# Hedgehog linear attention on one core: K and Q weights folded together, and another order of the first loads

## The chip, the cores and the metric

The kernel runs on one core of one Trainium2 chip, in one launch. The metric is the device time of the core in microseconds (us). Its engines are TensorE (PE, with its weight loads shown as PEld), VectorE (DVE), ScalarE (ACT), GpSimd (POOL) and SyncE (SP). SP only issues transfers in this kernel; POOL issues four more (the head weights). The transfers of a core share 16 DMA engines.

## The reference

Two branches, A and B, run over the same input x (2048 tokens, 448 channels, 16 heads of 28) and are mixed by a gate. For each branch:

```python
q, k, v = split((x @ wqkv), 3)                     # 16 heads of 28
pq, pk = q @ w_phi[h], k @ w_phi[h]                # 28x28 for each head
phi_q = concat(softmax(pq), softmax(-pq))          # 56 features
phi_k = concat(softmax(pk), softmax(-pk))
kv, z = phi_k.T @ v, phi_k.sum(tokens)
o = (phi_q @ kv) / (phi_q @ z + 1e-6)
branch = o @ wo
out = g * branch_A + (1 - g) * branch_B            # g = sigmoid(x . gate_w)
```

All is float32. x and the weights reach TensorE as a high part and a low part (the value rounded, and what the rounding left), and three of the four products are summed.

## The kernel before, in words

The 2048 tokens are 16 tiles of 128; two tiles make a pair of x. A projection half (one tile, one of the two branches b) is 11 matmuls: 448 channels are three chunks of 128 and one of 64, and the last chunk carries the low part of x in its upper half. So V of a tile is 22 matmuls, K 22, Q 22.

K and Q are never projected with the raw weights. The head matrices `w_phi` are first multiplied into the raw K and Q weights ("fold"), so that x times the folded weights gives pk and pq at once. `load_wt` loads the transposed raw weights of K or Q of a branch in four transfers, one for each partition quarter (28 partitions each, four runs of 2 KB per partition). `fold` multiplies four groups of heads in 32x32 tiles of the array into the four PSUM banks F, DVE transposes F (L338) to `ft`, ACT casts four column blocks to the high part (`rk` for K, `rq` for Q), and DVE or POOL subtracts the low part.

`steps()` writes the order of the work out by hand. It sets the order of TensorE strictly; for all other engines a planner (class `Plan`) takes each step with its cost, latency and `ahead` and lets every engine take the most urgent step that is ready. The planner counts no more than eight transfers in flight. What it emits is then fixed: every engine runs its instructions in order. At the start the steps are

- `V01`: V of tiles 0 and 1, the terms taken as weights arrive (`v_first`, L413; tile 1 uses the bank of K),
- `FK` 0, x of pair 1 (`x1`), V of tile 2, `FK` 1, loads of the raw Q weights (`wq`), V of tile 3, x of pair 2,
- `FQ` 0 and 1 with V of tile 4, K of tiles 0 and 1, then a loop over pairs: K, Q, `S` (softmax of Q in another layout, by a round trip through DRAM), `kv` (L467, sums K features times V), V of the pair after.

After the loop come the products with `kv` and the output projection (L597). The loads before all this, in SP's queue: x of pair 0 (512 KB), eight V weight chunks (225 KB each, `load_wv`), four raw K loads, x of pair 1, four raw K loads, x of pair 2, eight raw Q loads. Ten warm-up matmuls and thirty small ones (L606 and L609) run ahead of everything. `split_x` and `split_wv` make the high part on ACT (L269) or DVE and the low part on DVE or POOL (L266). `load_wp` brings the head weights `wp` by POOL. `k_soft` makes the K features: ACT copies K from PSUM to `pk`, DVE takes maxima and sums, POOL subtracts and scales. `hand_over` makes one buffer's users wait for another's.

Memory is shared in time: the raw V weights, x of pair 1 and the raw Q weights lie in `re`, which later holds the K features; the raw K weights lie in `rt`, later the Q features.

## Time and profile before

| what | value |
|---|---|
| median of 3 runs | 344.81 us |
| lowest and highest run | 343.89, 345.26 us |
| span of the profiled execution, first to last instruction | 343.6 us |
| TensorE busy | 333.2 us (97%) |
| DVE, POOL, ACT busy | 283.8, 241.0, 145.3 us |
| granted clock of TensorE | 0.999 |
| moved by DMA | 55.21 MB, mean 161 GB/s |

The profiled execution's own device time is not listed beside its span; the times of the runs lie 0.3 to 1.7 us above that span.

In the profile a line such as `L380 PE MATMUL K<-rk,rx 128*128 128x432 f32 x22` names the kernel's line, the engine, the operation, the output and inputs, the shapes and the count; in the timeline it has start and length in us ahead of it, and in brackets the idle time before it with what ended that. In a table by stretch, each engine's busy time stands with its count of instructions, then the granted clock, the share of the 16 DMA engines that was busy, and GB/s. In the chain of waits each row has start, length and who held the chain.

### The profile page before, as it was taken

To read this page: it belongs to the slowest core of one execution; us is meant where nothing else is said; L and a number is where in the kernel's file an instruction comes from. 1 tells how busy PE (TensorE), PEld (TensorE's weight loads), DVE (VectorE), ACT (ScalarE), POOL (GpSimd) and SP (SyncE) were. 2 spreads that over 40 slices of the span, in tenths; PEclk is the share of its full clock that TensorE was granted. 3 is DMA by queue.
4 is the path that set the end of the run, shared out by engine and by line. 5 is a ranking of instruction groups with operands and counts; after the bars stand their busy time and mean duration, and the time that the engine had idled before them with its cause. 6 is when DMAs were issued, how large, how long until landed. Compare 5 with 4: busy or idle time off the path is not lost.

```text
span 343.6 us, 9382 instructions
## 1 busy us (share of the span) xinstructions
PE 333.2 (97%) x4032; PEld 298.5 (87%) x4032; DVE 283.8 (83%) x342; ACT 145.3 (42%) x219; POOL 241.0 (70%) x195
## 2 busy tenths in 40 slices
PE   7979999999999999999999999999899999999995
PEld 6857799899999999999999999999688888888895
DVE  3548788897987979879899799986699999999870
ACT  4527665444444526446236344242043343433231
POOL 3003287999999969997987986895088678788400
PEclk9999999999999999999999999999999999999999
DMA  7998720650477486386446332377955644241011
GB/s 243 223 193 184 208 74 27 189 170 1 110 280 211 136 306 213 113 259 245 129 117 246 97 80 86 94 265 246 317 191 192 202 156 164 93 175 56 30 53 53
DMA packets 29488, 55.21 MB, mean 161 GB/s; under 512 B 4304, under 2 KB 23248, under 8 KB 27144
## 3 DMA queue, kind: packets, MB, share of 16 engines
q1 hardware_dynamic: 29320, 54.52, 51.0%
q8 instruction: 31, 0.51, 0.6%
q0 software_dynamic: 128, 0.12, 0.1%
q14 instruction: 9, 0.07, 0.1%
HBM read 32.00 MB, written 24.22 MB: 164 GB/s over the span
## 4 chain that ended last, share of the span: by engine, by line
PE 91%; DMA 5%; issue 1%; ACT 1%; SPq 1%; POOL 0%; POOLq 0%; ACTq 0%
PE K L380 20%; PE O L597 20%; PE Q L380 20%; PE VA L380 10%; PE VB L380 9%; PE N L549 6%; PE T L467 4%; DMA re<-in_xt 4%; PE F L334 2%; DMA re<-in_wv 2%; SPq L272 1%; ACT rx L269 0%; POOL re L266 0%; ACT re L269 0%; POOLq L266 0%
## 5 line engine op out<-in xcount | busy, mean ns | idle before, releaser
L380 PE MATMUL Q<-rq,rx 128*128 128x432 f32 x352 | 72.2, 359 | 1.1 <-issue 1.1
L380 PE MATMUL K<-rk,rx 128*128 128x432 f32 x352 | 72.2, 360 | 0.0
L597 PE MATMUL O<-rk,rx 128*128 128x448 f32 x336 | 70.4, 368 | 0.0
L380 PEld LDWEIGHTS Q<-rq,rx 128*128 128x128 f32 x352 | 66.0, 188 | 4.7 <-issue 1.2
L597 PEld LDWEIGHTS O<-rk,rx 128*128 128x128 f32 x336 | 62.6, 188 | 8.1 <-issue 1.6
L380 PEld LDWEIGHTS K<-rk,rx 128*128 128x128 f32 x352 | 65.9, 188 | 3.4 <-issue 0.2
L266 POOL TENSOR_TENSOR re<-re,sm 128x896 f32<-128x896 f32 x32 | 53.9, 1707 | 7.6 <-DVE sm L456 7.4
L269 ACT ACTIVATE re<-re 128x896 f32<-128x896 f32 x32 | 30.5, 953 | 31.9 <-POOL re L266 31.7
L455 DVE TENSOR_REDUCE sm<-re 128x32 f32<-128x896 f32 x32 | 33.8, 1071 | 4.4 <-ACT re L269 4.4
L266 POOL TENSOR_TENSOR rt<-qmn,ru 128x896 f32<-128x896 f32 x16 | 28.2, 1764 | 11.7 <-DMA ed<-rt 7.3
L380 PE MATMUL VA<-rv,rx 128*128 128x450 f32 x154 | 34.5, 372 | 1.4 <-ACT rx L269 1.4
L507 DVE TENSOR_REDUCE qsm<-rt 128x32 f32<-128x896 f32 x32 | 33.5, 1056 | 0.6 <-ACT rt L269 0.4
L380 PE MATMUL VB<-rv,rx 128*128 128x448 f32 x154 | 33.5, 365 | 0.0
L269 ACT ACTIVATE rt<-ru 128x896 f32<-128x896 f32 x16 | 15.3, 953 | 40.7 <-issue 17.3
L380 PEld LDWEIGHTS VA<-rv,rx 128*128 128x128 f32 x154 | 28.5, 189 | 4.5 <-ACT rx L269 1.7
L380 PEld LDWEIGHTS VB<-rv,rx 128*128 128x128 f32 x154 | 29.0, 188 | 2.3
L512 DVE STREAM_TRANSPOSE rt<-rt 128x2048 f32<-128x2048 f32 x13 | 29.6, 2278 | 1.6 <-POOL rt L266 1.5
L266 POOL TENSOR_TENSOR re<-pk,mx 128x896 f32<-128x896 f32 x16 | 27.9, 1746 | 2.7 <-DVE mx L448 2.7
L266 POOL TENSOR_TENSOR rt<-rt,qsm 128x896 f32<-128x896 f32 x16 | 27.3, 1705 | 0.9
L266 POOL TENSOR_TENSOR re<-mx,pk 128x896 f32<-128x896 f32 x16 | 27.3, 1704 | 0.0
L269 ACT ACTIVATE pk<-K 128x896 f32<-128x896 f32 x16 | 14.8, 922 | 29.3 <-PE K L380 29.3
L569 POOL TENSOR_TENSOR rv<-rv,rd 128x896 f32<-128x896 f32 x14 | 23.9, 1704 | 1.1
(96 smaller groups left out, 462.9 us busy)
## 6 DMA issues: line engine op xcount, KB each, us to landing
ed<-rt SPq DMA_DIRECT2D x8, 1024.0 KB
qd<-ru SPq DMA_DIRECT2D x64, 112.0 KB
ru<-qd SPq DMA_DIRECT2D x16, 448.0 KB
re<-ed SPq DMA_DIRECT2D x5, 1024.0 KB
xraw<-in_xt SPq DMA_DIRECT2D x7, 512.0 KB
out<-re SPq DMA_DIRECT2D x16, 224.0 KB
wod<-wst SPq DMA_DIRECT2D x14, 224.0 KB
rk<-wod SPq DMA_DIRECT2D x2, 1568.0 KB
```

The source lines that it names most:

```text
L266: return lambda: ENG[eng].tensor_tensor(val(o), val(a), val(b), op)
L269: return lambda: A.activation(val(o), val(i), f, **k)
L272: return lambda: nc.sync.dma_start(o, i)
L334: nc.tensor.matmul(bank["F"][32 * o:32 * o + 32, q, g * P:(g + 1) * P], wpd[32 * q:32 * q + DH, b, g], wts[k][b][32 * q:32 * q + DH, g].re ...
L380: nc.tensor.matmul(bank[name][:, k, lo:hi], x[:, xc, o:o + P], w[l][:, c], start=i == 0, stop=i == len(XT) - 1)
L455: put("DVE", 2 * D, lambda s=s, e3=e3: V.tensor_reduce(sm[:, s], e3, AX.X, OP.add), [ke[s]], [("sm", t % 2, s)])
L467: nc.tensor.matmul(kvp()[32 * r:32 * r + DH + 1, b, g], vs[t % NV][:, b, h // 2, h % 2], es[t % NE][:, :, hs:hs + DH], start=(t == 0 and b ...
L507: put("DVE", 2 * D, lambda s=s, e3=e3: V.tensor_reduce(qsm[:, s], e3, AX.X, OP.add), [ke[s]], [("qsm", i, s)])
L512: add("DVE", 2.25, lambda: V.transpose(eTf[slot], eq.rearrange("p s a c f -> p (s a c f)")), ke, turned(slot))
L549: nc.tensor.matmul(bank["N"][32 * g:32 * g + 32, r, 2 * b * P:2 * b * P + 2 * P], kvt[32 * r:32 * r + 32, b, s, g], eTp[slots[0] // 2][32 ...
L569: put(eng, 2 * D, lambda: ENG[eng].tensor_tensor(mid["o", n % 3].rearrange("p (c a f) -> p a c f", c=4, a=8), ctv()[:, :, i, :, :DH], rd[: ...
L597: nc.tensor.matmul(bank[pb][:, 0, :D], a, w, start=i == 0, stop=i == len(terms) - 1)
```

## The change

- Raw K and Q weights are folded together. A fold now takes one branch b and every second head group (gh): its matmuls have 256 moving columns, 128 of K and 128 of Q. There are still four folds, of half as many matmuls. Each fold makes K's and Q's high and low parts; K's are given priority on ACT, and low parts alternate between DVE and POOL.
- The transfers of the raw weights of partition quarters 0 and 1 stay on SP's queue, those of quarters 2 and 3 go on ACT's queue and start after the last V chunk is cast. K and Q weights of branch 0 are loaded first, then those of branch 1. `rt` and `re` become one tile `ret`, so that the raw weights of both lie in one range.
- x of pair 0 is loaded as chunk 0, then (after the first V chunk) chunks 1 to 3, and split by chunks on ACT, DVE and POOL. `v_first` takes its 11 terms in another order.
- x of pair 1 is split on ACT with one low half on DVE and one on POOL; its load comes ahead of the raw weights. x of pair 2 is split by POOL alone.
- The head weights come in eight transfers instead of four.
- The bank of K is tracked by halves; tile 0's K output is copied in two halves. K of tile 3 runs ahead of kv(0,1). The second half of V of tile 4 runs ahead of K of tile 0.

The diff, cut to its core:

```diff
-    yield from (("V01", 0, 0, 1), ("V01", 1, 0), ("V01", 1, 1), ("FK", 0), ("x1",), ("V", 2), ("FK", 1), ("wq", 0), ("wq", 1), ("V", 3), ("x", 2))
-    yield from (("FQ", 0), ("V", 4, 0), ("FQ", 1), ("later",), ("K", 0), ("V", 4, 1), ("K", 1), ("wo_rows",))
-    yield from (("Q", 0), ("S", 0, JIT % 3 - 1), ("K", 2), ("Q", 1), ("S", 1, (JIT - 1) % 3 - 1), ("kv", 0, 1), ("K", 3), ("V", 5))
+    yield from (("V01", 0, 0, 1), ("x1",), ("V01", 1, 0), ("V01", 1, 1), ("wq", 0), ("x", 2), ("wq", 1), ("V", 2, 0), ("F", 0, 0), ("V", 2, 1), ("F", 0, 1))
+    yield from (("V", 3, 0), ("F", 1, 0), ("V", 3, 1), ("V", 4, 0), ("F", 1, 1), ("later",), ("V", 4, 1), ("K", 0), ("K", 1), ("wo_rows",))
+    yield from (("Q", 0), ("S", 0, JIT % 3 - 1), ("K", 2), ("Q", 1), ("S", 1, (JIT - 1) % 3 - 1), ("K", 3, 0), ("kv", 0, 1), ("K", 3, 1), ("V", 5))
...
+    def load_x0():
+        for i, (lo, hi) in enumerate(((0, 1), (1, 4))):
+            if i:
+                load_wv(0, 0)
+            add("SP", 0.4, dma(xraw[:, lo:hi], xd[lo * P:hi * P, :2 * P].rearrange("(c p) t -> p c t", p=P)), [], [("x0raw", i)], lat=3, kb=184 * (hi - lo), ahead=60.0 - 20 * i)
+
+    def split_x0():
+        n, t, f = 0, xs[0], xs[0].bitcast(F32)
+        h, l = [[(k, n, i) for i in range(2)] for k in ("x", "xl")]
+        put("ACT", 2 * P, act(t[:, 0], xraw[:, 0]), [("x0raw", 0)], [("x0h", 0)])
+        low_part("DVE", 2 * P, t[:, 4], xraw[:, 0], f[:, 0], [("x0raw", 0), ("x0h", 0)], [("x0l", 0)])
+        put("DVE", 6 * P, lambda: V.tensor_copy(t[:, 1:4], xraw[:, 1:]), [("x0raw", 1)], [("x0h", i) for i in (1, 2, 3)])
+        low_part("DVE", 2 * P, t[64:P, 3], xraw[64:P, 3], f[64:P, 3], [("x0raw", 1)], [("x0h", 3)])
+        low_part("POOL", 4 * P, t[:, 5:7], xraw[:, 1:3], f[:, 1:3], [("x0raw", 1), ("x0h", 1), ("x0h", 2)], [("x0l", i) for i in (1, 2)])
...
-            add("POOL", 1.0, lambda q=q: G.dma_start(wp[32 * q:32 * q + DH], wphi[DH * q:DH * q + DH]), [], [("wp", q)], lat=3)
+            for b in range(2):
+                i = wphi[:, b, q].rearrange("(g d) f -> d g f", g=4)
+                add("POOL", 0.6, lambda q=q, b=b, i=i: G.dma_start(wp[32 * q:32 * q + DH, b], i), [], [("wp", q)], lat=3)
...
+        rows = (wkt, wqt)[k][b].rearrange("(q g d) c -> q d g c", q=4, d=DH)
+        for q in (0, 2, 1, 3):
+            o = wts[32 * q:32 * q + DH, k, b]
+            eng = nc.scalar if q > 1 else nc.sync
+            add("SP", 0.2, lambda eng=eng, o=o, i=rows[q]: eng.dma_start(o, i), [("vh", 3, 1)] if q > 1 else [], [("wt", k, b, q)], lat=2, kb=260)
+
+    def fold(b, gh):
+        n = 2 * b + gh
         def mm():
+            for l in range(2):
+                g = 2 * l + gh
                 for o in range(4):
                     for q in range(4):
+                        nc.tensor.matmul(bank["F"][32 * o:32 * o + 32, q, 256 * l:256 * l + 256], wpd[32 * q:32 * q + DH, b, g],
+                                         wts[32 * q:32 * q + DH, :, b, g].rearrange("p k (j o i) -> p o k j i", o=4, i=32)[:, o],
                                          start=True, stop=True)
+        add("PE", 1.4, mm, [("wpd",), *[("wt", k, b, q) for k in range(2) for q in range(4)]], ["F"])
+        f = ft[n % 2]
+        add("DVE", 2.25, lambda: V.transpose(f.rearrange("p k j f u -> p (u k j f)"), bank["F"].rearrange("p k n -> p (k n)")),
+            ["F"], [ftk[n % 2]])
+        for k, (wh, wl) in enumerate(((wkh, wkl), (wqh, wql))):
+            for j in (0, 2):
+                h, l = (x[:, j:j + 2, b, :, gh::2] for x in (wh, wl))
+                s = f[:, k, j:j + 2, :FD]
+                key = "kq"[k]
+                add("ACT", 0.6, act(h, s), [ftk[n % 2]], [(key, "h", b, gh, j)], ahead=2.0 * (k == 0))
+                e = ("DVE", "POOL")[j // 2]
+                add(e, {"DVE": 0.6, "POOL": 1.0}[e], tt(e, l, s, h.bitcast(F32), OP.subtract), [ftk[n % 2], (key, "h", b, gh, j)], [(key, "l", b, gh, j)], two=e == "DVE")
...
+        parts = [([(c, i, c)], [("x0h", c), ("v" + "hl"[i], c, b)]) if i < 2 else ([(4 + c, 0, c)], [("x0l", c), ("vh", c, b)])
+                 for c, i in ((0, 0), (0, 1), (1, 0), (0, 2), (1, 1), (2, 0), (1, 2), (2, 1), (3, 0), (2, 2), (3, 1))]
...
-            split_x(a[0], 0, 2 * P, "POOL", after=[("k", "h", 3, 0)] if a[0] == 2 else [])
+            split_x(a[0], 0, 2 * P, "POOL", "POOL" if a[0] == 2 else "ACT")
...
+            if a[0]:
+                plan.hand_over([("wvr", c, b) for c in range(4) for b in range(2)], [("wt", k, 1, q) for k in range(2) for q in range(4)])
+            for k in range(2):
+                load_wt(k, a[0])
```

More of the change, by code (lines that the diff above doesn't have):

```diff
@@ L324, in load_wt @@
     def load_wt(k, b):
-        for q in range(4):
-            o, i = wts[k][b][32 * q:32 * q + DH], {"K": wkt, "Q": wqt}[k][b].rearrange("(g q d) c -> q d g c", q=4, d=DH)[q]
-            add("SP", 0.4, dma(o, i), [], [("wt", k, b, q)], lat=2, kb=460, ahead=3.0 * (k == "K" and b == 0))
-    def fold(k, b, wh, wl, key, low):
+        rows = (wkt, wqt)[k][b].rearrange("(q g d) c -> q d g c", q=4, d=DH)
[3 more added lines that the diff above has]
+            add("SP", 0.2, lambda eng=eng, o=o, i=rows[q]: eng.dma_start(o, i), [("vh", 3, 1)] if q > 1 else [], [("wt", k, b, q)], lat=2, kb=260)
@@ L336, in mm @@
                                          start=True, stop=True)
-        add("PE", 1.95, mm, [("wpd",), *[("wt", k, b, q) for q in range(4)]], ["F"])
-        add("DVE", 2.25, lambda: V.transpose(ft[b].rearrange("p q g j f -> p (q g j f)"), bank["F"].rearrange("p k n -> p (k n)")),
-            ["F"], [ftk[b]])
-        for j in range(4):
-            h, l = (x[:, j, b].rearrange("p f (g q) -> p q g f", q=4) for x in (wh, wl))
-            s = ft[b][:, :, :, j, :FD]
-            add("ACT", 0.75, act(h, s), [ftk[b]], [(key, "h", j, b)])
-            e = low[j]
-            add(e, {"DVE": 0.85, "POOL": 1.35}[e], tt(e, l, s, h.bitcast(F32), OP.subtract), [ftk[b], (key, "h", j, b)], [(key, "l", j, b)], two=e == "DVE")
+        add("PE", 1.4, mm, [("wpd",), *[("wt", k, b, q) for k in range(2) for q in range(4)]], ["F"])
@@ L347, in wo_rows, with wkeys @@
+    def wkeys(k, bs):
+        return [(k, h, b, gh, j) for h in "hl" for b in bs for gh in range(2) for j in (0, 2)]
     def wo_rows():
@@ L627, in hedgehog_mix @@
     load_x(1)
-    for b in range(2):
-        load_wt("K", b)
-    first("DVE", 0.1, lambda: V.memset(bank["K"][:, :, FZ:FZ + H], 0.0), ["K"])
+    first("DVE", 0.1, lambda: V.memset(bank["K"][:, :, FZ:FZ + H], 0.0), [("K", 0), ("K", 1)])
     for i, v in enumerate(vs):
@@ L677, in hedgehog_mix @@
                 spill(*a)
-        elif what == "FK":
-            fold("K", a[0], wkh, wkl, "k", ("DVE",) * 4)
-        elif what == "FQ":
-            fold("Q", a[0], wqh, wql, "q", ("DVE", "POOL") * 2)
+        elif what == "F":
+            fold(*a)
         elif what == "kv":
```

82 lines of the change are left out of this document (41 added, 41 removed).

## The prediction

> **What bounds the kernel now.** The page first: how much of the span TensorE works, and whose work the chain of waits follows.
>
> ```profile
> span 343.6 us, 9382 instructions
> PE 333.2 (97%) x4032; PEld 298.5 (87%) x4032; DVE 283.8 (83%) x342; ACT 145.3 (42%) x219; POOL 241.0 (70%) x195
> PE 91%; DMA 5%; issue 1%; ACT 1%; SPq 1%; POOL 0%; POOLq 0%; ACTq 0%
> ```
>
> The chain is TensorE's for 91%; the only other large part is 5% of DMA. The chain in order of time says where that lies.
>
> ```profile
> 9.23 12.26 DMA re<-in_xt
> 21.49 0.02 issue
> 21.51 0.64 ACT rx L269
> ...
> 46.09 2.23 PE VB L380 x11
> 48.32 4.32 PE K L380 x22
> ```
>
> All DMA in it lies before 22 us; from there TensorE follows itself with hardly a gap. So the effect of the change is read from the first 48 us. My mark is 48.3: then tile 0 of K and V of tiles 0 to 4 are done and tile 1 of K begins, and in the new order the same work is done there. One V half (11 matmuls) costs 2.23, a K tile (22) 4.32.
>
> The timeline shows what the 12.26 us transfer, x of pair 1, holds up.
>
> ```profile
> 5.35 0.72 PE L609 MATMUL F<-zero 32*32 32x32 f32 x60
> 6.00 0.48 PE L413 MATMUL VA<-rv,rx 128*128 128x450 f32 x1
> 7.08 0.58 ACT L269 ACTIVATE rv<-re 128x450 fp32r<-128x450 f32 x1 [1.53 <-DMA re<-in_wv]
> 14.66 2.39 PE L413 MATMUL K<-rv,rx 128*128 128x448 f32 x11
> 18.93 1.85 PE L334 MATMUL F<-rt,wpd 28*32 28x128 f32 x122 [0.93 <-DMA rt<-in_wkt]
> 22.20 2.52 PE L380 MATMUL VA<-rv,rx 128*128 128x450 f32 x11 [1.42 <-ACT rx L269]
> ```
>
> The first V matmul starts at 6.00, those of tiles 0 and 1 end at 17.05; then TensorE does one fold in pieces and waits for x until 22.20. Now the rate of the transfers by stretch (the last column is GB/s, before it the DMA share), and the issues with KB each:
>
> ```profile
> 2.00:10.00 8.00, 6.97 (x91) 6.18 (x90) 3.95 (x8) 3.60 (x8) 2.58 (x7) 1.00 1.01 315
> 24.00:33.00 9.00, 8.32 (x159) 6.97 (x158) 7.86 (x6) 5.98 (x11) 2.94 (x4) 1.00 0.92 186
> ```
>
> ```profile
> rt<-in_wkt SPq DMA_DIRECT2D x8, 224.0 KB
> re<-in_wqt SPq DMA_DIRECT2D x8, 224.0 KB
> re<-in_wv SPq DMA_DIRECT2D x4, 225.0 KB
> ```
>
> Full-height loads (x, V weights: 128 partitions) move 315 GB/s; raw weights, each on 28 partitions of one quarter, 186 at nearly the same DMA share. This is the disputed quantity.
>
> **The change part by part.**
>
> *First x and V weights by chunks.* A 128 KB chunk of x and one V chunk now lead the queue, so the first matmul's data come about 1 us sooner. At the start that is worth nothing: the warm-up matmuls hold TensorE until 6.00 (row at 5.35). Then 44 matmuls of 2.23/11 us are 8.9 us; the second V chunk is split at 7.08 as before, which leaves some 0.9 us of waiting after chunk 0's terms. The head weights, hidden until the first fold, now come in eight POOL transfers of 128-byte runs:
>
> ```profile
> q0 software_dynamic: 128, 0.12, 5.0%
> ...
> L319 POOL DMA_DIRECT2D wp<-in_wphi x4 | 2.2, 558 | 0.7 <-DVE wpd L320 0.7
> ```
>
> The first row is of the stretch 2 to 10 us: 128 packets took 5.0% of 16 engines' 8 us, 50 ns each. 28 x 4 x 8 = 896 packets would be 2.8 us of all engines if each cost as much, 0 if only bytes count (they are the same). I take 0.5, near the bytes' end. POOL's four more issues (2.2 us) lie in its idle time (below); the low part of x chunks 1 and 2 stands behind all eight on POOL (4.5 us from about 1.5), and its first matmul is due near 9. That cover goes if an issue costs half as much again. So V of tiles 0 and 1 ends at 6.0 + 8.9 + 0.9 + 0.5 = 16.3 rather than 17.05.
>
> *x of pair 1 ahead of the raw weights.* It now follows 2.5 MB: 3.0 MB by 315 GB/s from 2.0 us is 11.5, landing near 12.5 (1 us of landing is my estimate, between 0.5 and 2). Its splits, 0.64 each on ACT (row at 21.51) and low parts on DVE and POOL, are done by 15, under the V matmuls. The stall before 22.20 is gone; late next are the raw weights, since a fold now needs K and Q of its batch, 8 loads instead of 4.
>
> *Raw weights by two queues.* Half of the loads (partition quarters 2 and 3) leave SP's queue for ACT's; quarters 0 and 1 stay. If the 186 comes from the few partitions that one load reaches, two loads in flight on different quarters add up. Bounds: 186 as on one queue, 315 as for full height. I take 290, near the upper, as the DMA share of 0.92 at 186 fits engines that wait on their destination. Batch 0 (1.84 MB) is moved by 17.8 and landed at 18.8; x of pair 2 (0.52 MB) and batch 1 by 25.8, landed 26.8.
>
> The Trainium skill's page SBUF — State Buffer, section "Door 1: The DMA port swizzle", says that DMA rate goes by how many of 16 ports the partitions reach, that partition +32 is on the same port and +64 on another. By that rule quarters 0 and 1 share ports and SP and ACT get the two halves; the sum would be by 315 rather than 290 (fold pairs ready 0.5 and 1.2 us sooner). The 315 and 186 agree with it. The page DMA: Bandwidth & Descriptors, section "Issuing engines are not separate DMA queues", speaks against the change: queues share the same 16 DMA engines, so a second one saves issue time alone. By it the sum is the third rival below, at 186. No row of before has two queues on such loads.
>
> *Folding 256 wide.* A fold is 64 matmuls instead of 128 (512 instructions fewer in all with weight loads), and the same columns in total. In a stretch, for the fold's line alone (after the length, TensorE's busy time and count):
>
> ```profile
> 39.00:42.00 3.00, 2.10 (x128) 1.63 (x128) 1.00 0.63 177
> ```
>
> and the timeline around it:
>
> ```profile
> 37.11 2.31 DVE L338 STREAM_TRANSPOSE rt<-F 128x2048 f32<-128x2048 f32 x1
> 39.47 2.10 PE L334 MATMUL F<-re,wpd 28*32 28x128 f32 x128
> 39.52 0.54 ACT L269 ACTIVATE vs<-VA 128x448 f32<-128x448 f32 x1 [3.06 <-PE VA L380]
> 39.96 0.17 ACT L269 ACTIVATE glog<-VA 128x1 f32<-128x1 f32 x1
> ```
>
> A fold is 2.10, 16.4 ns a matmul; the 60 warm-up matmuls of 32 columns took 0.72, 12.0 each. A straight line through both gives 22.3 ns at 256 columns, 1.43 for 64. Bounds: 1.05 (cost by instruction) and 2.10 (cost by column); I take 1.5. The next fold waits for the transpose, which starts with the fold's end, so that 2.4 us lie between two folds (37.11 to 39.47), against 2.23 of V matmuls between: 0.2 of stall each.
>
> *ACT, DVE and POOL behind the folds.* Rows of the casts and the issues:
>
> ```profile
> L269 ACT ACTIVATE rk<-rt 128x432 fp32r<-128x432 f32 x4 | 3.4, 964 | 0.9 <-DVE rt L338 0.9
> L266 POOL TENSOR_TENSOR rq<-rt,rq 128x432 fp32r<-128x432 f32 x2 | 2.7, 1364 | 7.8 <-ACT rq L269 7.8
> ```
>
> ```profile
> 1.24 4.13 SPq L272 DMA_DIRECT2D re<-in_wv x8
> SPq L272 <- DMA rt<-in_wkt: 7.9, 8, 2.3
> ```
>
> Per fold ACT has 4 casts of 0.96; eight of the 16 low parts go to POOL at 1.36, eight to DVE. POOL also takes both parts of pair 2's x: 2.65 for the low parts (row at 30.29, below) and, as more elements cost more there, an estimated 2 for the cast, done by 26, ahead of V of tile 4 at 30. ACT takes eight issues (0.52 each by 4.13/8) and stands still wherever one waits for an earlier transfer; SP did that 7.9 us for free, ACT would not. Four of them fall among the folds.
>
> *The sum, in time.* V half of tile 2 16.3 to 18.5. Fold 1 at 18.8 (weights) to 20.3; V; fold 2 at 22.7 (transpose) to 24.2; V; fold 3 at 26.8 (weights) to 28.3; V, V; fold 4 at 32.8 to 34.3; V to 36.5; K tile 0, first half, to 38.7. Its second half needs fold 4's K parts: transposed 36.7, two casts 38.6, POOL's low part 40.0, if ACT were free. But ACT, from 22.7 on, has 14 casts (13.4), four V outputs and two gates (2.5; rows at 39.52 and 39.96) and four issues (2.1): 40.7. That binds; with POOL's part 42.1, and K ends at 44.3 against 48.3: 4.0 gained.
>
> *After it.* Tile 0's K output in two halves adds one cast's start on ACT; K of tile 3 ahead of kv(0,1) moves 4.3 us of TensorE work and no cost, and gives POOL time there. POOL must follow:
>
> ```profile
> 29.89 0.31 POOL L647 MEMSET rt<- 128x256 f32 x1 [25.31 <-PE F L334]
> 30.29 2.65 POOL L266 TENSOR_TENSOR rx<-xraw,rx 64x256 fp32r<-64x256 f32 x2
> 48.80 2.38 POOL L266 TENSOR_TENSOR re<-pk,mx 128x896 f32<-128x896 f32 x1
> 54.79 1.70 POOL L266 TENSOR_TENSOR re<-pk,mx 128x896 f32<-128x896 f32 x1 [1.94 <-DVE mx L448]
> 82.76 1.71 POOL L266 TENSOR_TENSOR re<-re,sm 128x896 f32<-128x896 f32 x1
> 85.32 1.78 PE L467 MATMUL T<-re,vs 128*29 128x56 f32 x128
> 56.00:86.00 30.00, 29.79 (x320) 27.67 (x323) 25.56 (x34) 14.27 (x18) 28.92 (x19) 1.00 0.38 111
> ```
>
> POOL's last scaling ends 0.85 before kv(2,3) starts, and from 48.8 it idles only 3.0 (1.94 before 54.79, 1.1 after 56). K's end is 4.0 sooner and nothing of the folds is left for POOL after it, so POOL starts some 2.5 sooner, and up to 2.5 + 3.0 + 0.85 = 6 us of gain can pass; 4.0 does. The sum is made against the profiled span: 343.6 - 4.0 = 339.6. The runs' median of 344.81 lies 1.2 above that span, so the time is **340.8**.
>
> **The rivals.**
> *All at the good end:* loads at 315, fold 1.05 to 1.5, Q casts behind K's. Folds 3 and 4 follow the transposes and V alone, K ends near 42.1: gain 6.2, 338.6. For it: POOL idle until 29.9 takes its share; against: POOL's limit of 6.
> *ACT is held by its own issues:* if waits like SP's (up to 2.3 at a time) hold ACT by 2.6 more, the casts end at 43.4: gain 1.4, 343.4. For it: SP waited for eight of eight raw loads; against: ACT issues them after the V splits, when the earlier transfers have mostly landed.
> *The rate stays at 186:* the change doesn't do what it says. Batch 1 lands at 11.5 + 1.7 + 3670/186 + 1.0 = 33.9, fold 3 starts there instead of 26.8, and with a fold at its upper 2.10 the end is 33.9 + 2 x 2.1 + 2 x 2.23 + 2.4 + 1.9 + 1.4 + 2.2 = 50.4: 2.1 later, 346.9; with 1.5 it is 49.2, 345.7. It costs more than before because Q weights, formerly folded last (the fold at 39.47 is theirs), are now needed before K. The point of decision is about 196 GB/s, where fold 3 starts at 32.9 and, with the 1.5, K ends at 48.3.
>
> **How the numbers follow.** Forecast 0.52, all good 0.13, ACT held 0.17, rate unchanged 0.18. 0.5%, about what a measurement of this kernel can tell from no change, is 1.7 us: faster is below 343.1, slower above 346.5. Faster: 0.52 + 0.13 + 0.03, the light end of ACT held; slower: 0.13 of the unchanged rate; same: the rest, 0.19. The range runs from 338.3, just past the good end, to 346.0, which holds ACT held and the mild unchanged rate, and leaves out some 0.18. The forecast alone: 339.4 to 342.4.
>
> **What the profile after would show.** Right: 270 GB/s or more while raw weights come; no DMA of x in the chain after 12 us; first fold near 19, with 64 matmuls in about 1.5 us; tile 1 of K at 44; DMA issues on ACT's queue without long waits; kv(2,3) unstalled. Wrong: raw weights at 190; fold 3 waiting for DMA past 32; ACT idle on issues; or TensorE waiting for POOL at 60 to 90 us, which gives the gain back.

## The result, and the profile after

The changed kernel is slower: 356.31 us median of 4 runs (354.1 to 357.38) against 344.9 us for the kernel before on the same chip, a ratio of 1.0323 with a 95% interval of 1.0281 to 1.0365, that is 11 us lost. The prediction was 340.8 us, in a range of 338.3 to 346.0. Below, a ratio is always to the kernel before on the same chip, and "lost" is the ratio less 1, times 345 us. Some executions were disturbed and longer, among them the profiled ones of E5, E9 and E11; the ratios leave them out (the medians do not), and from these three profiles only the order of events is read.

The page of the changed kernel, with the engines' busy times and the granted clock by fortieths of the span:

```profile
span 352.2 us, 8890 instructions
PE 336.2 (95%) x3776; PEld 298.9 (85%) x3776; DVE 285.8 (81%) x334; ACT 144.3 (41%) x219; POOL 255.2 (72%) x207
PEclk9969998999999999999999999999999999999999
```

TensorE executes 256 matmuls fewer than before and is busy 3 us longer. The clock row says why that can be: it shows a 6 in the third slice and an 8 in the seventh, where the kernel before had 0.999 as its mean. Two stretches of the span show the first of these in numbers (length, then PE, PEld, DVE, ACT and POOL busy, clock, DMA share, GB/s):

```profile
16.00:26.00 10.00, 6.64 (x23) 5.48 (x23) 0.85 (x2) 2.58 (x6) 2.24 (x3) 0.66 0.95 220
20.00:24.00 4.00, 4.00 (x12) 3.54 (x11) 0.00 (x0) 0.55 (x1) 0.00 (x0) 0.50 0.93 227
```

The timeline, TensorE and ACT (ACTq is ACT's sequencer issuing a transfer):

```profile
14.29 1.17 PE L438 MATMUL K<-rv,rx 128*128 128x448 f32 x5
16.44 0.32 ACTq L345 DMA_DIRECT2D ret<-in_wqt  x1
16.81 1.15 ACT L268 ACTIVATE rx<-ret 128x512 fp32r<-128x512 f32 x2 [3.25 <-DMA ret<-in_wkt]
19.14 0.17 ACT L268 ACTIVATE glog<-K 128x1 f32<-128x1 f32 x1
19.36 2.61 PE L438 MATMUL K<-rv,rx 128*128 128x448 f32 x6 [3.90 <-ACT glog L268]
21.77 3.92 PE L406 MATMUL VA<-rv,rx 128*128 128x450 f32 x11
27.01 1.44 PE L354 MATMUL F<-ret,wpd 28*32 28x256 f32 x58 [0.77 <-DMA ret<-in_wqt]
```

This is the first loss. ACT's third raw-weight issue stands until 16.44, released by an earlier raw-weight transfer. Behind it on ACT stand the cast of x of pair 1, the V copies and the gate's exponential of tile 1, which reads one half of the bank of K. The sixth V matmul of tile 1 writes the other half and, by the profile, waits for that exponential, 3.90 us; why five such matmuls could run ahead of it and the sixth could not, no run shows. Then a V half takes 3.92 instead of 2.5, at a clock of 0.50, and the first fold's main part starts at 27.01, when its last quarter has landed.

TensorE's wait is the visible part, but the page's chain of waits does not run through it. In this stretch the chain follows the raw weights alone, up to the third fold:

```profile
12.06 8.61 DMA ret<-in_wkt
20.76 8.93 DMA ret<-in_wqt
29.70 5.91 DMA ret<-in_wqt
35.75 1.40 PE F L354 x55
```

The first of these transfers is the first that ACT issues, and it comes late: SP issued its four of batch 0 between 6.54 and 10.47. The last is the last that ACT issues, at 29.70. Fold 3 begins when it has landed, at 35.75.

The second loss is at the other end of the fold chain:

```profile
42.93 1.49 PE L354 MATMUL F<-ret,wpd 28*32 28x256 f32 x64
43.15 1.90 DVE L265 TENSOR_TENSOR rk<-ret,rk 128x432 fp32r<-128x432 f32 x1 [0.27 <-ACT rk L268]
44.98 2.25 DVE L265 TENSOR_TENSOR rq<-ret,rq 128x432 fp32r<-128x432 f32 x1
47.15 2.31 DVE L359 STREAM_TRANSPOSE ru<-F 128x2048 f32<-128x2048 f32 x1
52.64 6.02 PE L406 MATMUL K<-rk,rx 128*128 128x432 f32 x22 [3.63 <-ACT pk L268]
61.56 1.74 PE L406 MATMUL Q<-rq,rx 128*128 128x432 f32 x8
```

Fold 4 is done at 44.4, its transpose begins at 47.15, behind two low parts of fold 3 on DVE (the rows at 43.15 and 44.98). K's second half waits 3.63 and then runs 22 matmuls in 6.02 us instead of 4.5. The first Q matmul starts at 61.56; in the kernel before, this row stood at 52.47:

```profile
52.47 4.49 PE L380 MATMUL Q<-rq,rx 128*128 128x432 f32 x22
```

That is 9.1 later, and the span is 8.6 longer (352.2 against 343.6): all of the loss arises ahead of the first Q. From there to the end the changed kernel takes 290.6 us and the kernel before 291.1, with TensorE busy for 286.5 and 286.4. TensorE's longest wait there is 0.48, for POOL, in the changed kernel, and 1.07 in the kernel before; so POOL's limit, which the prediction watched, does not matter here.

### The profile page after: what moved, and what is told of

Its sections match the earlier page's. It is cut to its first block, busy times and chain, and to the rows that moved or that the text cites. A ratio compares the mean times of both kernels' runs of the same rounds, so it can differ in the third digit from the quotient of the medians.

```text
span 352.2 us, 8890 instructions
## 1 busy us (share of the span) xinstructions
PE 336.2 (95%) x3776; PEld 298.9 (85%) x3776; DVE 285.8 (81%) x334; ACT 144.3 (41%) x219; POOL 255.2 (72%) x207
## 4 chain that ended last, share of the span: by engine, by line
DVE 31%; POOL 25%; PE 18%; DMA 13%; issue 6%; ACT 4%; SPq 2%; POOLq 0%; DVEq 0%; ACTq 0%
POOL ret L265 19%; PE O L627 10%; DVE ret L542 7%; DVE sm L485 5%; DMA ret<-in_wqt 4%; DVE rv L590 3%; POOL rv L599 3%; DMA ret<-in_wkt 2%; PE N L579 2%; DVE qmx L512 2%; DVE ru L265 2%; ACT ret L268 2%; DVE qsm L537 2%; DMA ed<-ret 2%; SPq L271 2%
## 5 line engine op out<-in xcount | busy, mean ns | idle before, releaser
L268 ACT ACTIVATE ret<-ret 128x896 f32<-128x896 f32 x48 | 45.6, 952 | 58.3 <-POOL ret L265 58.2
L265 POOL TENSOR_TENSOR ret<-ret,sm 128x896 f32<-128x896 f32 x32 | 53.9, 1705 | 10.0 <-DVE sm L486 10.0
L485 DVE TENSOR_REDUCE sm<-ret 128x32 f32<-128x896 f32 x32 | 34.0, 1077 | 7.4 <-ACT ret L268 7.4
L542 DVE STREAM_TRANSPOSE ret<-ret 128x2048 f32<-128x2048 f32 x16 | 36.5, 2282 | 4.3 <-POOL ret L265 4.1
L537 DVE TENSOR_REDUCE qsm<-ret 128x32 f32<-128x896 f32 x32 | 33.3, 1059 | 1.3 <-ACT ret L268 1.0
L265 POOL TENSOR_TENSOR ret<-qmn,ru 128x896 f32<-128x896 f32 x16 | 28.2, 1763 | 8.3 <-DMA ed<-ret 4.2
L265 POOL TENSOR_TENSOR ret<-pk,mx 128x896 f32<-128x896 f32 x16 | 27.3, 1704 | 8.7 <-DVE mx L478 8.7
L268 ACT ACTIVATE ret<-ru 128x896 f32<-128x896 f32 x16 | 15.2, 953 | 34.1 <-issue 18.9
L265 POOL TENSOR_TENSOR ret<-ret,qsm 128x896 f32<-128x896 f32 x16 | 27.3, 1706 | 0.9
L265 POOL TENSOR_TENSOR ret<-mx,pk 128x896 f32<-128x896 f32 x16 | 27.3, 1706 | 0.0
```

The source lines that it names most:

```text
L265: return lambda: ENG[eng].tensor_tensor(val(o), val(a), val(b), op)
L268: return lambda: A.activation(val(o), val(i), f, **k)
L485: put("DVE", 2 * D, lambda s=s, e3=e3: V.tensor_reduce(sm[:, s], e3, AX.X, OP.add), [ke[s]], [("sm", t % 2, s)])
L537: put("DVE", 2 * D, lambda s=s, e3=e3: V.tensor_reduce(qsm[:, s], e3, AX.X, OP.add), [ke[s]], [("qsm", i, s)])
L542: add("DVE", 2.25, lambda: V.transpose(eTf[slot], eq.rearrange("p s a c f -> p (s a c f)")), ke, turned(slot))
```

## The experiments

**E1: all raw weights on SP's queue.** The order of quarters stays 0, 2, 1, 3.

```diff
-            eng = nc.scalar if q > 1 else nc.sync
-            add("SP", 0.2, lambda eng=eng, o=o, i=rows[q]: eng.dma_start(o, i), [("vh", 3, 1)] if q > 1 else [], [("wt", k, b, q)], lat=2, kb=260)
+            add("SP", 0.4, dma(o, rows[q]), [], [("wt", k, b, q)], lat=2, kb=260)
```

> The changed kernel with all raw K and Q weights issued on SP's queue again, in the same order of quarters; nothing else differs. Theory A (ACT is held by its own issues: it stands still at an issue until an earlier transfer has landed, so casts that TensorE needs come late): TensorE's 3.9 us wait in V of tile 1 goes, V of tile 2 starts by 17 instead of 21.8 and at full clock, and the time falls by 4 to 8 us, to 348 to 352. Theory B (the loss is that a fold needs all eight loads of its batch at the old rate; which queue issues them is beside the point): the first fold still starts its main part near 27, the time stays at 354 to 358, or rises a little if the second queue gave some rate.

Measured: 349.79 us, ratio 1.0101 (1.0033 to 1.0169): 3.5 lost instead of 11.1. The second queue thus costs some 7.7 us (give or take 2.8, by the two intervals).

```profile
15.71 1.47 PE L437 MATMUL K<-rv,rx 128*128 128x448 f32 x6 [0.26 <-ACT glog L268]
21.15 1.45 PE L353 MATMUL F<-ret,wpd 28*32 28x256 f32 x58 [0.46 <-DMA ret<-in_wqt]
29.85 2.43 PE L353 MATMUL F<-ret,wpd 28*32 28x256 f32 x62 [0.34 <-DMA ret<-in_wqt]
46.37 6.19 PE L405 MATMUL K<-rk,rx 128*128 128x432 f32 x22 [3.29 <-ACT pk L268]
55.46 4.49 PE L405 MATMUL Q<-rq,rx 128*128 128x432 f32 x22
```

The wait for ACT falls from 3.90 to 0.26 and the first fold starts 5.9 sooner, although one queue carries everything. Fold 3 starts 5.9 sooner as well, and the first Q 6.1 sooner: in the profiles the gain is the arrival of the weights. The one queue even moves more, 225 GB/s from 12 to 20 us and 246 from 20 to 26, where the two moved 197 and 222. The wait ahead of K's second half, with the slow matmuls behind it, stays.

**E2: the second queue in the kernel before.** Quarters 2 and 3 of its raw loads on ACT's queue, nothing else.

```diff
-            add("SP", 0.4, dma(o, i), [], [("wt", k, b, q)], ...)
+            eng = nc.scalar if q > 1 else nc.sync
+            add("SP", 0.4, lambda eng=eng, o=o, i=i: eng.dma_start(o, i), [("vh", 3, 1)] if q > 1 else [], [("wt", k, b, q)], ...)
```

> The kernel before with one part of the change alone: raw weights of partition quarters 2 and 3 go on ACT's queue, after the seventh-to-last V cast as in the change. Theory A: ACT stalls at its issues in the first 30 us, casts of x and V outputs come late, 3 to 8 us slower than before (348 to 353). Theory B: the queue does not matter, within 1 us of before; and if the second queue raises the rate, x of pair 1 lands before 21.5 and the time falls by 1 to 3 us.

Measured: 347.6 us, ratio 1.0086 (1.0044 to 1.0129), 3.0 lost.

```profile
20.87 2.54 PE L335 MATMUL F<-rt,wpd 28*32 28x128 f32 x122 [1.55 <-DMA rt<-in_wkt]
22.38 5.47 ACTq L328 DMA_DIRECT2D re<-in_wqt  x3
27.90 0.55 ACT L269 ACTIVATE vs<-VA 128x448 f32<-128x448 f32 x1 [9.11 <-DMA xraw<-in_xt]
```

Three issues take ACT's sequencer 5.47 us, and ACT does no work for 9.11 us. TensorE feels it in both ways: it waits 1.44 and then 1.55 us for raw K weights (in the kernel before 0.20 and 0.93), with the rest of the fold at a clock of 0.55 behind that, and later 0.67 for a transpose, which by the page's chain stands behind ACT's late casts. The second queue does harm by itself, at the lower end of what was expected.

**E3: TensorE kept busy in its two waits.** Sixteen and fifteen matmuls on zeros are put where the changed kernel's TensorE stood still (ahead of the sixth V matmul of tile 1, and ahead of K's second half), to see whether the clock is what costs.

```diff
+            if (b, list(ts), pos) == (1, [1], 5):
+                add("PE", 0.0, lambda: keep("F", 16), [("zero",)], ["F"])
...
+                    if a[0] == 0 and b:
+                        add("PE", 0.0, lambda: keep("O0", 15), [("zero",)], ["O0"])
```

> The changed kernel with unused matmuls on zeros where TensorE waits 3.9 and 3.6 us: 16 in V of tile 1 behind its fifth term, 15 between the two halves of K of tile 0. They do no work of the computation. Theory C (the halved granted clock after the two waits is a loss of its own): the clock stays at 1.0, V of tile 2 takes 2.3 instead of 3.9 and K after the second wait 4.5 instead of 6.0, and the time falls. The first is hidden, since the first fold waits for weights until 27 anyway, so I expect 1.5 to 2 us in all, 354.5; if both count, 4 us, 352.5; if the clock does not matter, no change or up to 1 us slower.

Measured: 357.17 us, ratio 1.0335 (1.0271 to 1.04): no gain.

```profile
20.23 2.41 PE L406 MATMUL VA<-rv,rx 128*128 128x450 f32 x11
26.33 2.31 PE L354 MATMUL F<-ret,wpd 28*32 28x256 f32 x58 [1.82 <-DMA ret<-in_wqt]
28.57 4.13 PE L406 MATMUL VB<-rv,rx 128*128 128x448 f32 x11
```

The clock did hold (the V half 2.41 instead of 3.92), but the time went into waiting for the weights, and the clock fell there instead. So filling this wait saves nothing as long as the weights behind it are late. The second filling waited 2.20 us for DVE itself, began at 51.43, ran at about half clock and pushed K's second half to 56.43 from 52.64. What the clock costs there this run does not tell.

**E4: the transfers alone.** The raw weights' 16 loads in seven ways one after the other, and no other work; the program computes nothing of the reference.

> Only transfers, none of the computation: seven stages, each of eight loads of 224 KB, the next stage after the last has landed. 1: raw weights on SP's queue, partition quarters 0,1,2,3,0,1,2,3. 2: quarters 0,2,1,3 twice, on SP. 3: quarters 0,1 on SP and 2,3 on ACT, in turn, as in the change. 4: quarters 0 and 1 alone, on SP and ACT. 5: loads of 128 partitions on SP. 6: the same on SP and ACT. 7: quarter 0 alone on SP. Theory D (what limits a load of 28 partitions is the partitions that it reaches, and quarters 0 and 1 share that, 2 and 3 the other half): stages 1, 4 and 7 near 186 GB/s, stage 3 near 300, stage 2 above 1, stages 5 and 6 above 300. Theory E (it is the transfer engines or the queue): stages 1, 2, 3, 4 and 7 alike, or stage 4 as fast as stage 3.

Measured in the middle of each stage (length, busy time of DVE and POOL, clock, DMA share, GB/s): quarters 0, 1, 2, 3 on SP; 0, 2, 1, 3 on SP; 0 and 1 on SP beside 2 and 3 on ACT; quarters 0 and 1 alone on both queues; then, in GB/s and without their rows, full height on SP 308, full height on both 371, and quarter 0 alone 183.

```profile
20.00:28.00 8.00, 0.00 (x0) 0.00 (x0) 1.00 0.92 193
31.50:38.50 7.00, 0.00 (x0) 0.00 (x0) 1.00 0.91 219
42.00:48.50 6.50, 0.00 (x0) 0.00 (x0) 1.00 0.88 232
52.00:60.00 8.00, 0.00 (x0) 0.00 (x0) 1.00 0.94 182
```

What partitions are in flight together does limit the rate, as the prediction supposed: quarters 0 and 1 on two queues move no more (182) than quarter 0 on one (183). But both halves together move 232, not 290 to 315, and one queue that alternates between them already moves 219. The second queue is worth 13 GB/s; from the first issue to the last landing the eight loads take 10.2 us on the one queue and 10.0 on the two.

**E5: DVE's order at the end of the chain.** E1's kernel, and the planner gives the transpose priority.

```diff
-            ["F"], [ftk[n % 2]])
+            ["F"], [ftk[n % 2]], ahead=3.0)
```

> The changed kernel with all raw K and Q loads on SP's queue, so that ACT issues none, and in the planner a priority for DVE's transpose of a fold, so that it runs ahead of the Q low parts of the fold before. Nothing else differs. With the loads alone on SP's queue the profile shows K of tile 0 waiting 3.29 us for the copy of its first half at 43, and its second half then running at a clock of 0.61 (6.19 us instead of 2.2). Theory (the tail of the fold chain on DVE is the rest of the loss): the wait falls below 1.5 us and the clock stays at 1, 4 to 6 us less than 349.8, so 344 to 346, no slower than before the change. Rival (the tail is set by the weights' arrival, not by DVE's order): the last fold ends where it did and the time stays within 1.5 us of 349.8. Rival (DVE's Q low parts, pushed back, hold up the first Q tile): the wait moves to the first Q matmuls, 347 to 349.

Measured: 346.73 us, ratio 1.0039 (1.0 to 1.0078): 1.3 lost instead of E1's 3.5; the difference of 2.1 is about as large as the two intervals leave uncertain, but has the sign expected. In the profile two rows stand next to each other:

```profile
42.09 2.20 POOL L265 TENSOR_TENSOR rk<-ret,rk 128x432 fp32r<-128x432 f32 x1
44.35 1.06 PE L405 MATMUL K<-rk,rx 128*128 128x432 f32 x4 [0.50 <-POOL rk L265]
```

K's first half (branch 0) waits inside for POOL's low part of fold 3, which belongs to branch 1 and which it does not read. The wait ahead of K's second half is still there, so the theory, which had it below 1.5 and the time at 344 to 346, is not borne out as it stands.

**E6: POOL instead of ACT as the second queue.**

```diff
-            eng = nc.scalar if q > 1 else nc.sync
+            eng = nc.gpsimd if q > 1 else nc.sync
```

> The changed kernel with the raw loads of partition quarters 2 and 3 on POOL's queue instead of ACT's; SP keeps quarters 0 and 1, so there are still two queues, and ACT issues none. Theory (the loss is ACT held by its own issues, not the second queue): the 3.9 us wait of TensorE for ACT at 15.5 is gone, since ACT's casts run freely; POOL stands still at its issues instead, which delays low parts of x of pair 1 and of the folds: 347 to 352, nearer to the 349.8 of one queue than to the 356.3. Rival (two queues as such slow the start, by contention): the time stays within 2 us of 356.3. Rival (any engine held between 12 and 29 us costs the same): POOL's low part of x of tile 1 delays V of tile 3 and K, 354 to 358.

Measured: 357.01 us, ratio 1.0348 (1.0273 to 1.0423). The last rival's number came, by another way than it said:

```profile
17.82 0.60 POOL L345 DMA_DIRECT2D ret<-in_wkt  x1
27.59 1.03 POOL L313 CAST rx<-xraw 128x1024 fp32r<-128x1024 f32 x1 [9.17 <-DMA xraw<-in_xt]
28.57 0.60 POOL L345 DMA_DIRECT2D ret<-in_wkt  x1
36.91 1.46 PE L354 MATMUL F<-ret,wpd 28*32 28x256 f32 x58 [2.97 <-DMA ret<-in_wqt]
38.30 3.99 PE L406 MATMUL VB<-rv,rx 128*128 128x448 f32 x11
```

The time that was expected, 347 to 352, did not come. TensorE's wait for ACT in V of tile 1 does fall, to 1.18. But here it is not the work that stands behind an issue, but the issue behind the work: POOL's next raw load comes after the cast of x of pair 2, which waits 9.17 us for its data. The weights of fold 3 are 7 us later than in E1 (36.91 against 29.85). An issue on an engine that computes went wrong in both directions, on both engines tried. That two queues as such cost the time, the first rival, is not ruled out by the number (357.01 against 356.31); but alone (E4) two queues moved no less than one, and the rows here show the issues.

**E7: x of pair 1 ahead of the raw weights, in the kernel before.** The one part of the change whose stall the prediction saw in the profile. For this the first raw K loads also lose their priority in the planner, and the split of x no longer waits for V of tile 1 (not shown in the cut).

```diff
-... ("V01", 1, 1), ("FK", 0), ("x1",), ("V", 2), ("FK", 1), ...
+... ("V01", 1, 1), ("x1",), ("V", 2, 0), ("FK", 0), ("V", 2, 1), ("FK", 1), ...
```

> The kernel before the change, with one part alone: the load of x of pair 1 ahead of the raw K weights, with tile 2's first V half between the two, one after the other, ahead of the first fold. Theory (the prediction's step: x of pair 1 in time is worth the stall ahead of 22.2): TensorE no longer waits for x; the first fold's weights come 1.6 us later, but 2.2 us of V run ahead of it: 1 to 3 us less than 344.8, so 342 to 344. Rival (the weights set the end anyway: every raw load is only pushed back by 512 KB): within 1 us of 344.8. Rival on the other side (x in front of the raw weights makes a wait ahead of the first fold that is long enough to halve the clock): 346 to 349.

Measured: 346.03 us, ratio 0.9999 (0.9951 to 1.0047): nothing.

```profile
27.89 1.42 PE L334 MATMUL F<-rt,wpd 28*32 28x128 f32 x52 [3.66 <-issue]
29.24 4.30 PE L380 MATMUL VA<-rv,rx 128*128 128x450 f32 x11
```

The waits for x are gone, and one of 3.66 us ahead of the second fold's last matmuls takes their place, with a V half at half clock behind it. The profile names no releaser for it; that it is the raw weights, pushed back by 512 KB, is inferred from the sequence. So the 1.42 us seen in the kernel before were not to be had in this way; that the transfers as a whole were the bound there fits, and E12 bears it out.

**E8 to E11: taking the fold chain's waits away one by one.** All keep E5's one queue and its priority for the transposes. E8 lays out the folded weights with the branch outermost:

```diff
-    wkh, wkl = (rk[:, i].rearrange("p (c b f h) -> p c b f h", c=4, b=2, f=FD) for i in range(2))
+    wkh, wkl = (rk[:, i].rearrange("p (b c f h) -> p c b f h", c=4, b=2, f=FD) for i in range(2))
```

(and `wqh`, `wql` alike).

> The kernel of the last step (changed kernel, raw loads on SP's queue alone, transposes of the folds with priority on DVE), with one more edit: the folded weights lie in memory with branch b outermost, so that a cast of two chunks of one branch no longer spans the other branch's columns. In the last profile the eighth K matmul of tile 0, branch 0, began at 44.35, right after POOL's low part of fold 3 (branch 1, which it does not read) ended at 44.29. Theory (a false dependency by overlapping spans makes K of branch 0 wait for branch 1's folds): K's first half starts about 2 us sooner, with no wait for POOL inside; but the second half still waits for the last fold, so the end moves by 0 to 2 us: 344.5 to 346.7. Rival (no such dependency): the first half waits as before, 346.7 within 1. Rival on the other side: an earlier first half leaves TensorE a longer wait ahead of the second, up to 5 us, after which its clock is halved for longer: 347 to 349.

Measured: 347.72 us, ratio 1.0132 (1.0079 to 1.0185).

```profile
42.24 2.33 PE L405 MATMUL K<-rk,rx 128*128 128x432 f32 x11
47.34 6.23 PE L405 MATMUL K<-rk,rx 128*128 128x432 f32 x22 [2.77 <-ACT pk L268]
```

K's first half now runs in one piece: the wait for branch 1 was a dependency by overlapping spans only. But the second half, which needs fold 4, does not come sooner: TensorE stands 2.77 us ahead of it and then runs at half clock. That is the last rival: 4.6 us lost, more than E5's 1.3. Not all of it arises there: in this profile the first fold waits 1.13 and 0.37 us for weights, and the V half behind it takes 4.05 at 23.81 where E1's took 2.49.

E9 adds fold 4 one V half sooner, K of tile 0 copied in one piece, and truer costs for the planner:

```diff
-    ... ("V", 3, 1), ("V", 4, 0), ("F", 1, 1), ("later",), ("V", 4, 1), ("K", 0), ...
+    ... ("V", 3, 1), ("F", 1, 1), ("later",), ("V", 4, 0), ("V", 4, 1), ("K", 0), ...
-        if t:
+        if True:
             put("ACT", 2 * D, act(pk, p4), ...
```

> The same with three more edits: fold 4 directly after the one V half that follows fold 3 (both V halves of tile 4 come behind it instead of one ahead), K of tile 0 copied in one piece again, so that its second half no longer waits for a copy of the first, and the planner's costs of the folds' casts and low parts set to what the profiles show (ACT 0.95, DVE 1.5, POOL 1.8 us). Theory (the fold chain's tail, fold to transpose to casts to low parts, about 6 us, only needs enough V work behind the last fold): 6.7 us of TensorE work (two V halves, K's first half) stand behind fold 4, K's second half starts unstalled near 42 to 43, clock at 1: K of tile 0 ends near 44.5 against 48.3 before, 341 to 343, faster than before by 0.5 to 1%. Rival (weights for fold 3, near 30, and the transposes set the end): fold 4 waits for its bank, the time is 343.5 to 345.5, no change from before. Rival (POOL, with the first K features now due sooner, gives the gain back in the loop): TensorE waits for POOL between 55 and 90, 344 to 346.

Measured: 347.61 us (343.5 to 353.41), ratio 1.0088 (1.0048 to 1.0128), 3.0 lost. K of tile 0 ran through without a wait, but fold 4 had moved into one:

```profile
39.67 2.37 PE L353 MATMUL F<-ret,wpd 28*32 28x256 f32 x64 [2.41 <-DVE ret L358]
```

Transpose 3 needs the buffer of fold 1 and DVE comes to it late, so the second theory (weights and transposes set the end) holds for this kernel. E10 keeps the layout and the copy in one piece, has one V half of tile 4 ahead of fold 4 again, gives each fold a buffer of its own, puts both V halves of tile 2 ahead of fold 1 and lets ACT cast x of pair 2, whose load thereby moved ahead of batch 1 of the raw weights:

```diff
-    ... ("V", 2, 0), ("F", 0, 0), ("V", 2, 1), ("F", 0, 1)) ... ("V", 3, 0), ("F", 1, 0), ("V", 3, 1), ("V", 4, 0), ("F", 1, 1), ...
+    ... ("V", 2, 0), ("V", 2, 1), ("F", 0, 0), ("V", 3, 0), ("F", 0, 1)) ... ("V", 3, 1), ("F", 1, 0), ("V", 4, 0), ("F", 1, 1), ...
-        f = ft[n % 2]
+        f = ft[n]
```

> The changed kernel with all raw loads on SP's queue, branch b outermost in the folded weights, K of tile 0 copied in one piece, and the chain of the folds rearranged so that TensorE has work at each point where it stood still: both V halves of tile 2 ahead of fold 1 (its weights landed at 22.4, TensorE came at 20.2); a transposed buffer of its own for each fold, so that a transpose no longer waits until the low parts of the fold before the last are done; DVE's order: transpose 3 ahead of the low parts of K of fold 2, transpose 4 ahead of most Q low parts; x of pair 2 cast by ACT; fold 4 after one V half of tile 4. Theory (the rest of the loss is TensorE standing still 1 to 3 us at three places of the fold chain, each followed by some 4 us at half clock): no wait over 1 us between 17 and 45, clock 0.99 to 1, K of tile 0 ends at 42 to 45 against 48.3 before, 339.5 to 342.5. Rival (DVE and POOL are the bound of the chain: four transposes of 2.3 and eight low parts of 1.6 to 2.2 on DVE fill 24 to 46): K's second half waits 1 to 4 us, the clock drops once, 343 to 346. Rival (what is gained is given back in the loop, where POOL limits): first Q by 4 us sooner than before, TensorE waits for POOL at 55 to 90, 342.5 to 345.

Measured: 352.77 us, ratio 1.0205 (1.0154 to 1.0256), 7.1 lost, worse than any of its rivals said.

```profile
33.24 2.26 PE L353 MATMUL F<-ret,wpd 28*32 28x256 f32 x58 [0.51 <-DMA ret<-in_wqt]
48.51 1.63 PE L411 MATMUL K<-rk,rx 128*128 128x432 f32 x7 [2.96 <-DVE rk L265]
```

Fold 1 had no wait any more; the weights of fold 3 came at 33.2 instead of 29.8, and the last low part of K on DVE late. E11 mended both (x of pair 2 behind the raw weights, K's low parts ahead of Q's):

```diff
-... [], [(kr,)], lat=2, kb=512)
+... [], [(kr,)], lat=2, kb=512, ahead=-60.0 * (p == 2))
```

> The kernel of the last step, mended where its profile showed waits: x of pair 2 comes behind all raw weights again (in the last kernel it came ahead of batch 1, whose last quarter then landed at 33.2 instead of 29.8), and DVE makes the low part of K of fold 4 ahead of all Q low parts but one (there it stood behind one, and K's second half waited 2.96 for it). Steps: both V halves of tile 2, fold 1, V, fold 2, V, fold 3, V half of tile 4, fold 4, V, K of tile 0. Theory (the chain's waits and the half clock after them are the rest of the loss): waits of about 1.5 near 31 (x of pair 2) and 1 to 1.5 ahead of K's second half, none over 2, clock 0.99 or more; the first Q matmul near 49 to 51 against 52.5 before: 341 to 344. Rival (two waits of 1.5 are enough to halve the clock): one to two stretches of 4 us at half clock, 345 to 349. Rival (DVE's and POOL's low parts run at half speed beside each other and end as late as in the last kernel): K's second half waits 3, 346 to 350.

Measured: 348.69 us (345.52 to 355.1), ratio 1.009 (1.0053 to 1.0126), 3.1 lost.

```profile
32.57 0.88 PE L413 MATMUL VA<-rv,rx 128*128 128x450 f32 x3 [1.04 <-ACT rx L270]
44.69 3.95 PE L413 MATMUL K<-rk,rx 128*128 128x432 f32 x11 [2.18 <-ACT rk L270]
```

Each mended wait came back at the next place: x of pair 2, then the casts of fold 4. No order tried with the joint fold beat the kernel before.

**E12: the order of quarters alone, in the kernel before.** This is the part of the change that E4 singled out, on one queue.

```diff
     def load_wt(k, b):
-        for q in range(4):
+        for q in (0, 2, 1, 3):
```

> The kernel before the change, with one edit: the raw loads of a matrix go in the order of partition quarters 0, 2, 1, 3 instead of 0, 1, 2, 3, all on SP's queue. Transfers alone moved 219 GB/s in that order and 193 in the other. Theory (the rate of the raw weights, not the second queue, is what is worth having): the first fold's wait of 0.93 falls below 0.5, x of pair 1 lands 0.5 sooner: 0.5 to 1.2 us less, at the limit of what can be told, 343.6 to 344.8 beside 345. Rival (no effect in place): the rate in the stretch 12 to 21 stays at 186 to 200 and the time too.

Measured: 343.34 us median of 12 runs (342.46 to 344.25) against 345.32, ratio 0.9926 (0.9897 to 0.9956): 2.5 us faster than before by the ratio, 2.0 by the medians, and the only version that beats both kernels. The second row is of the chain of waits.

```profile
24.00:33.00 9.00, 8.82 (x210) 6.88 (x208) 7.98 (x8) 7.78 (x12) 3.14 (x4) 1.00 0.83 216
9.15 10.45 DMA re<-in_xt
16.95 2.02 PE L334 MATMUL F<-rt,wpd 28*32 28x128 f32 x128
20.31 2.51 PE L380 MATMUL VA<-rv,rx 128*128 128x450 f32 x11 [1.34 <-ACT rx L269]
50.30 4.49 PE L380 MATMUL Q<-rq,rx 128*128 128x432 f32 x22
```

In the stretch where the kernel before moved 186 GB/s, 216 are moved; of the stretch that the expectation named, 12 to 16 us has 228 against 194, 16 to 21 no gain (212 and 215). The first fold runs in one piece from 16.95 to 18.97 (before: pieces until 20.8), x of pair 1 is used at 20.31 instead of 22.20, and the first Q starts at 50.30 instead of 52.47. The gain is larger than the 0.5 to 1.2 expected. The first fold's wait of 0.93 is gone, and x of pair 1, which is issued behind four raw loads, takes 10.45 us from issue to landing instead of 12.26; TensorE still waits for it, 1.34 instead of 1.42, but 1.9 us sooner.

## Why the prediction was wrong

The step that failed, in short: the sum put fold 3's weights at 26.8, from 290 GB/s and from issues on ACT that cost 0.52 each and no waiting. Fold 3 began at 35.75. That is 9 of the 13 us by which the first Q came later than forecast (61.56, where the kernel before had 52.47 and 4.0 were to be gained). Of these 9, 3 are left when ACT issues nothing (E1, 29.85) and 5.9 come with ACT's issues. The rest lies behind fold 3, in DVE's low parts and the clock, which had no terms.

*What bounds the kernel* was read rightly: the effect lay wholly ahead of the first Q matmul, and it passed to the end nearly undiminished (8.6 of 9.1), as a loss.

*First x and V weights by chunks*: V of tiles 0 and 1 was put at 16.3. Without ACT's hold (E1) it ended at 17.2, with it at 22.0. The first part of the step (matmuls from about 6) was right; the end was 0.9 off. The head weights came in 256 packets, not the 896 of the working.

*x of pair 1*: the stall went away, as said, but was worth nothing (E7): "late next are the raw weights" was the right sentence, and the price that the sum gave them, fold 1 at 18.8, was too low: its main part began at 21.15 in E1 and at 27.01 in the changed kernel.

*Raw weights by two queues*: this step failed first. 290 GB/s were taken, between bounds of 186 and 315; 220 are measured in the stretch 16 to 26, and 232 with nothing beside (E4). The argument, that two quarters add up, held in kind and not in size, and overlooked that the order of quarters gives most of it on one queue. With 220 in the prediction's own sum fold 3 starts at 30.9, close to E1's 29.85, and its deciding point of 196 still leaves a gain. So the rate alone does not explain a loss.

*ACT is held by its own issues*: this rival had the right mechanism and 2.6 us for it, a time of 343.4. The forecast put the waiting at nothing. The term measures 7.7 us (E1 against the changed kernel). The reason given against it, that the earlier transfers had mostly landed, was wrong, as the row at 16.44 shows: the third issue stood until then. And what was counted was only ACT's casts at the end of the chain. The hold took effect at its beginning. It stopped TensorE for 3.90 us, and it made the weights late: ACT's last issues came only at 25.22 and 29.22, so that fold 3 began at 35.75 in place of 29.85 on one queue (E1). The second is what counted, by the page's chain and by E3, where the first wait was filled and nothing was gained. How much of it is that an issue waits for an earlier transfer, and how much that it stands behind ACT's other work, no run separates.

*Fold*: 1.5 us for 64 matmuls was right (1.49). *ACT binds at 40.7*: it did not. The end of the chain was set by DVE, which the working gave only its transposes: each low part takes DVE 1.90 to 2.25 while POOL makes its own, against 0.93 for the same form at 41.10 with POOL idle, and DVE did two ahead of transpose 4, which began 2.7 us after its fold where the sum let it begin at once. POOL's cast of x of pair 2, put at 2, took 1.04. With the transpose moved forward (E5) about 2 us came back, no more than the two intervals leave uncertain.

*Tile 0's copy in halves, "no cost"*: K's second half waits for that copy by the profile, but the low parts ended at the same time (DVE's at 52.86), so this stays undecided.

*The clock* had no term at all. Behind waits of some 3 to 4 us TensorE ran at about half speed for some 4 us: 1.4 us more in a V half, 1.5 in K's 22 matmuls. In the kernel before no wait at the start was longer than 1.42 and the clock stayed at 0.999. The Trainium skill's page "TensorE: Matmul & The Clock Gate", in "Part 1: The HAM clock gate", says that the clock falls to half after an idle window of about 3.4 us, and that the windows run freely. The wait of 3.90 with the 0.50 behind it agrees; waits of 2.77 (E8, then 22 K matmuls in 6.23) and 2.97 (E6, then a fold at full speed and a V half in 3.99) are shorter than that window, so here the measurement goes further than the page.

What stays open: with ACT freed and DVE's order mended, the changed kernel is still 1.3 us (0 to 2.7) behind the kernel before, so perhaps level with it, and 3.8 behind E12, which has the same order of quarters. That a joint fold must have all of K's and Q's weights of a batch before it starts, with the transfers as the bound, is the likeliest cause, but not shown; E9 to E11, which moved the waits and did not remove them, speak for it, and no run had the joint fold without them.

## What to carry to other kernels

An issue of a transfer on an engine that computes can be a wait in that engine's order, in both directions: ask what stands behind the issue and what the issue stands behind. Before adding a queue, look at what the one queue's transfers reach, and change their order first; here it was one line, and worth 2 to 2.5 us. And where waits for one resource, here the transfers, follow each other, removing one of them gained nothing (E7), and faster transfers did (E12).

## What the runs showed of the hardware

- Transfers to 28 partitions moved 183 GB/s when all went to one quarter, and 182 when they went to quarters 0 and 1 by two queues; in the order 0, 1, 2, 3 on one queue 193; alternating between the halves 219 on one queue and 232 on two; to all 128 partitions 308 on one and 371 on two. The Trainium skill's page "SBUF — State Buffer", section "Can I just issue two DMAs to hit both halves?", says no: two transfers at once gave 6% over one. Here the measurement goes against it: transfers to both halves gave 27% over one quarter with two queues (232 to 183) and 20% already with one (219 to 183).
- TensorE's waits of 0.93 and 1.42 in the kernel before, with a fold of 1.85 between them, left the clock at 1.00; those of 2.77 to 3.90 us named above did not. Nor did two waits of 1.44 and 1.55 with only two short matmuls between them (E2, 0.55 from 21 to 24 us).
- A low part (a subtraction of 128x432) took DVE 0.93 alone and 1.50 to 2.25 beside POOL's, and POOL 1.60 to 2.21, all in the changed kernel.
